# An attention and feed-forward kernel replayed from a step list: the same operations and buffers in a newly fitted order

## The chip, the cores and the metric

The kernel runs on one core of one Trainium2 chip. The metric is the device time of one execution in microseconds, by its median over several executions. A profile shows one single execution, and its span is some 1.8 us shorter than the time of the same execution.

## The reference

Attention with RMS-normed q and k over 8 batches, 12 heads, 448 rows and 64 columns, then a feed-forward block on the 3584 x 768 result:

```python
q_n, k_n = rmsnorm(q, g_q), rmsnorm(k, g_k)
attn = softmax(q_n @ k_n.T / sqrt(64))          # per batch and head
x = (attn @ v).transpose(0, 2, 1, 3).reshape(3584, 768)
h = x @ w_in                                    # 3584 x 2048
g = h * erf(softplus(h))
out = g @ w_out                                 # 3584 x 768
```

## The kernel before

The kernel first records some 2800 operations. Each has a number, the engines that may do it, and the keys that it reads and writes, from which its dependencies follow. Then it replays a step list. A step is a letter for the engine (P TensorE, V VectorE, A ScalarE, G GpSimd, S the sync engine's transfer queue) and the number of the operation. `^n` adds a wait for operation n. `z2*6` is six dummy matmuls on zeros into idle PSUM bank 2.

```python
for step in SCHEDULE.split() or [...]:
    e, what = step[0], step[1:]
    if e == "z":
        bank, n = what.split("*")
        for _ in range(int(n)):
            nc.tensor.matmul(idle[int(bank)], zs[:, 0:P], zs, start=True, stop=True)
        continue
    what, *after = what.split("^")
    o = plan.ops[int(what)]
    o.inst = o.fn(e)
    for d in [*o.sync, *(plan.ops[int(i)] for i in after)]:
        tc.add_manual_dep(o.inst.ins, d.inst.ins.name, must, reason="order")
```

So each engine works through its own steps in the order of the list, whatever else is ready. One unit of four heads begins with four loads into a buffer `raw`, of which there are two. Squares and reduces give the norms:

```python
# four loads per unit: q and k rows 0-383 (384 KB each), q and k rows 384-447
add("S", "ld_raw" if x < 2 else "ld_raw_last", (b, 2 * u, x),
    lambda e, ...: nc.sync.dma_start(dst, src), writes=[key])
# ... twice per unit:
add("G", "sq",  ..., nc.gpsimd.tensor_tensor(sq, part, part, op=ALU.mult), reads=ks, writes=["sq"])
add("V", "red", ..., nc.vector.tensor_reduce(ss[...], sq, ...), reads=["sq"], writes=[("st", si)])
```

The feed-forward products go through two PSUM banks `f` in turn. Each bank is evicted to `ob` (of which there are two as well) and stored:

```python
add("P",  "f2", ..., products, reads=gk + [("wo", n0 // 2)], writes=[("f", fi)])
add("VA", "eo", ..., lambda e: copy(e, osb[oi], fp[:, :JS]), reads=[("f", fi)], writes=[("ob", oi)])
add("S",  "st", ..., lambda e: nc.sync.dma_start(dst, sr), reads=[("ob", oi)])
```

"VA" means that the list chooses VectorE or ScalarE. The first four heads of the first batch are loaded in pairs instead (operations 13 to 20); they are normed, and transposed on TensorE (the first such transpose is P39).

The softmax here doesn't subtract the row's maximum and nothing guards it: scores larger than these inputs give would overflow.

## Time and profile before

| | before |
|---|---|
| time, median of 3 | 472.06 us (471.39 to 472.33) |
| span of the profiled execution | 467.7 us |
| busy TensorE, VectorE, ScalarE, GpSimd | 96, 69, 83, 42% |
| granted TensorE clock | 1.0 |
| TensorE idle | 19.0 us |

A row of the table of costliest groups has, after the bar, busy time and mean ns, and after the second bar the idle time of the engine just before these instructions, with what ended most of it. Two rows, the squares on GpSimd and the reduces on VectorE:

```profile
L320 POOL TENSOR_TENSOR sq<-raw 128x896 f32<-128x896 f32 x42 | 70.5, 1678 | 39.9 <-DMA raw<-in_q_dram 19.0
...
L322 DVE TENSOR_REDUCE st<-sq 128x14 f32<-128x896 f32 x42 | 45.4, 1081 | 16.5 <-POOL sq L320 16.1
```

The squares wait 19.0 us for raw loads, the reduces 16.1 us for squares.

### The profile page before, as it was taken

How to read it: one execution, taken by the hardware profiler on the slowest of the kernel's cores; microseconds unless marked ns; L12 is line 12 of the kernel's file. 1: busy time of each engine (PE TensorE's matmuls, PEld its weight loads, DVE VectorE, ACT ScalarE, POOL GpSimd, SP SyncE). 2: the span in 40 equal slices, each digit the busy share in tenths (PEclk: the TensorE clock that was granted, in tenths of full speed). 3: DMA queues.
4: the chain of work that ended last, by engine and by line, in shares of the span. 5: the costliest groups of instructions: out<-in, count | busy, mean ns of one | idle time of the engine just before them, and what ended most of it. 6: DMA issues, size and time to landing. Idle time of an engine off the chain costs nothing.

```text
span 467.7 us, 7365 instructions
## 1 busy us (share of the span) xinstructions
PE 448.7 (96%) x2579; PEld 221.1 (47%) x2579; DVE 323.2 (69%) x507; ACT 387.7 (83%) x511; POOL 195.1 (42%) x329
## 2 busy tenths in 40 slices
PE   8888999899999998999989999999999999999996
PEld 3334344434554444544454445544455444655663
DVE  3797777798679964797758975698758943284711
ACT  3988999999898988978898897988789886998510
POOL 4467775657562582614552365515370420000000
PEclk9999999999999999999999999999999999999999
DMA  7988999969872447507591377716743022110121
GB/s 166 270 189 163 233 195 173 190 141 189 173 183 85 118 99 217 140 2 189 131 239 52 86 134 168 169 52 154 162 130 87 2 39 67 52 35 18 68 85 68
DMA packets 107893, 59.77 MB, mean 128 GB/s; under 512 B 58576, under 2 KB 107856, under 8 KB 107856
## 3 DMA queue, kind: packets, MB, share of 16 engines
q1 hardware_dynamic: 101440, 52.45, 45.9%
q0 software_dynamic: 5440, 6.29, 9.2%
q10 hardware_dynamic: 976, 0.56, 0.5%
q8 instruction: 20, 0.33, 0.3%
q14 instruction: 17, 0.14, 0.1%
HBM read 45.61 MB, written 11.01 MB: 121 GB/s over the span
## 4 chain that ended last, share of the span: by engine, by line
PE 75%; DVE 7%; DMA 7%; ACT 4%; SPq 3%; POOL 2%; issue 2%; DVEq 0%; POOLq 0%
PE f L657 28%; PE f L707 26%; PE o L543 13%; PE s L466 6%; DMA raw<-in_q_dram 2%; DMA out_dram<-ob 2%; ACT e L509 2%; POOL sq L320 2%; DMA vl<-in_v_dram 2%; PE s L518 1%; DVE g L684 1%; SPq L387 1%; DVE h L275 1%; DVE qk L336 1%; DMA vs<-in_v_dram 1%
## 5 line engine op out<-in xcount | busy, mean ns | idle before, releaser
L657 PE MATMUL f<-xT,w_in_sb 128*128 128x448 bf16 x768 | 163.2, 353 | 3.5 <-DVE h L275 2.9
L509 ACT ACTIVATE e<-s 128x896 bf16<-128x896 f32 x144 | 126.9, 914 | 20.2 <-PE s L466 19.0
L657 PEld LDWEIGHTS <-w_in_sb 128*128 128x128 bf16 x768 | 72.0, 98 | 76.6 <-issue 15.1
L320 POOL TENSOR_TENSOR sq<-raw 128x896 f32<-128x896 f32 x42 | 70.5, 1678 | 39.9 <-DMA raw<-in_q_dram 19.0
L275 DVE COPY h<-f 128x448 f32<-128x448 f32 x101 | 62.0, 620 | 22.7 <-PE f L657 21.4
L606 DVE TENSOR_TENSOR xT<-o,r 64x448 bf16<-64x448 f32 x84 | 52.2, 621 | 35.3 <-ACT r L602 31.4
L543 PE MATMUL o<-e,vm 128*128 128x448 bf16 (+1 forms) x324 | 67.2, 354 | 1.7 <-DVE xT L595 1.4
L707 PE MATMUL f<-w_out_sb,g 128*128 128x384 bf16 x384 | 66.8, 326 | 1.3 <-DVE ob L275 1.2
L707 PE MATMUL f<-w_out_sb,godd 128*128 128x384 bf16 x384 | 65.0, 326 | 2.4 <-DVE ob L275 2.4
L322 DVE TENSOR_REDUCE st<-sq 128x14 f32<-128x896 f32 x42 | 45.4, 1081 | 16.5 <-POOL sq L320 16.1
L275 DVE COPY ob<-f 128x384 f32<-128x384 f32 (+1 forms) x46 | 25.3, 551 | 44.5 <-PE f L707 41.4
L600 ACT ACTIVATE r<-o 64x448 f32<-64x448 f32 x84 | 45.2, 538 | 12.1 <-PE o L543 10.1
L672 ACT ACTIVATE sp<-sp 128x1792 f32<-128x1792 f32 x32 | 52.0, 1687 | 0.1
L668 ACT ACTIVATE sp<-h 128x1792 f32<-128x1792 f32 x31 | 50.4, 1686 | 1.1 <-DVE h L275 1.0
L707 PEld LDWEIGHTS <-godd 128*128 128x128 bf16 x384 | 37.4, 98 | 28.5 <-issue 3.8
L707 PEld LDWEIGHTS <-g 128*128 128x128 bf16 x384 | 37.1, 98 | 28.0 <-issue 3.1
L466 PE MATMUL s<-qT 64*128 64x448 bf16 x288 | 45.9, 356 | 3.8 <-ACT em L527 2.4
L336 POOL TENSOR_TENSOR qk<-raw,st 128x256 bf16<-128x256 f32 x42 | 30.1, 717 | 27.2 <-ACT st L327 18.6
L275 POOL COPY kp<-qT 64x64 bf16<-64x64 bf16 x71 | 21.0, 299 | 46.3 <-PE s L518 33.4
L543 PEld LDWEIGHTS <-vm 128*128 128x128 bf16 (+1 forms) x324 | 25.8, 100 | 30.4 <-issue 10.7
L336 DVE TENSOR_TENSOR qk<-raw,st 128x640 bf16<-128x640 f32 x42 | 36.3, 878 | 3.7 <-ACT st L327 3.3
L275 POOL CAST vm<-vl 128x384 bf16<-128x384 f32 x43 | 24.9, 580 | 30.9 <-DMA vl<-in_v_dram 13.5
(75 smaller groups left out, 441.7 us busy)
## 6 DMA issues: line engine op xcount, KB each, us to landing
vl<-in_v_dram SPq DMA_DIRECT2D x48, 192.0 KB, 3.8
out_dram<-ob SPq DMA_DIRECT2D x47, 192.0 KB, 2.2
raw<-in_k_dram SPq DMA_DIRECT2D x21, 384.0 KB, 4.6
raw<-in_q_dram SPq DMA_DIRECT2D x21, 384.0 KB, 4.7
w_in_sb<-in_moe_w_in_dram POOLq DMA_DIRECT2D x4, 768.0 KB, 7.5
w_out_sb<-in_moe_w_out_dram POOLq DMA_DIRECT2D x8, 384.0 KB, 5.2
out_dram<-ob SPq DMA_DIRECT2D x17, 96.0 KB, 2.2
vs<-in_v_dram SPq DMA_DIRECT2D x16, 96.0 KB, 3.8
```

Source lines behind the costliest of these rows:

```text
L275: return nc.scalar.copy(dst, src) if e == "A" else (nc.vector if e == "V" else nc.gpsimd).tensor_copy(dst, src)
L320: add("G", "sq", (b, 2 * u, x), lambda e, part=part: nc.gpsimd.tensor_tensor(sq, part, part, op=ALU.mult), reads=ks, writes=["sq"])
L322: add("V", "red", (b, 2 * u, x), lambda e, ss=ss, x=x: nc.vector.tensor_reduce(ss[:, 14 * x : 14 * x + 14], sq, axis=AX.X, op=ALU.add), re ...
L336: add(eng, "nq", (b, p, x), lambda e, g=g: (nc.vector if e == "V" else nc.gpsimd).tensor_tensor(qks[qi].rearrange("p g h d -> p h g d")[:, ...
L466: last = nc.tensor.matmul(st[:, i, :S], qT[r, c0 : c0 + P], qq[r], start=True, stop=True)
L509: add("A", "e", (b, p, s), lambda e, e_=e_, st=st: nc.scalar.activation(e_, st[:, :, :S], func=FN.Exp), reads=[("s", sl, 0), ("s", sl, 1), ...
L543: last = nc.tensor.matmul(dst, lhs, rhs, start=(s == 0), stop=(s == 3))
L606: add("V", "x", (b, p, i), lambda e, i=i, mine=mine: nc.vector.tensor_tensor(x[mine, p, :], o_ps[i][mine, :S], r[mine], op=ALU.mult), read ...
L657: last = nc.tensor.matmul(fp[:, :S], w_in_sb[:, kt, f * P : (f + 1) * P], x[:, kt, :], start=(kt == 0), stop=(kt == KT - 1))
L668: add("A", "sp1" if c == order[0] else "sp", (b, c), lambda e, c=c, h=h: nc.scalar.activation(sps[c], h, func=FN.Softplus), reads=[("h", c ...
L672: add("A", "erf1" if c == order[0] else "erf", (b, c), lambda e, c=c: nc.scalar.activation(sps[c], sps[c], func=FN.Erf), writes=[("sp", c, ...
L707: last = nc.tensor.matmul(fp[:, :JS], src[nt // 4][:, nt % 4, col : col + P], w_out_sb[:, nt, js], start=(nt == 0), stop=(nt == NF - 1))
```

## The change

The intent: the list was fitted anew, and the fit now charged work that is planned close behind the landing of a transfer. Only the step list differs. The whole list is replaced; here are its first lines and the stretch around the largest gap.

```diff
-A15 S16 G2 A13 S14 G7 S20 A19 G10 A17 S18 A12 S24 G1 G3 S23 G4 G11 S21 A29 G9 V30 S22 V0 S69 A31 G8 S125 A32 A34 V33
-S28 S27 z0*29 P39 V5 V35 S42 A40 S26 V41 A36 S25 A37 z2*6 P46 V38 P48 A47 S126 G60 A58 z4*3 P66 S124 P50 V67 A49
 [...]
-P1048 S1127 P1049 S1289 A1064 G1092 P1110 A1065 P1111 A1073 S1088 V1320 P1079 G1321^1320 A1072 P1071 S1292 P1112
-A1074 P1113 S1290 P1138 A1114 V1076 G1054 P1139 G1348 A1078 P1140 S1115 V1075 P1128 S1116 P1129 A1080 V846 S1291
-P1081 P1083 A1082 P1130 S1087 V1347 P1084 P1085 S1353 P1086 P1131 S1095 A1102 P1141 S1354 A1101 P1132 G1293 P1133
-S1356 P1142 A1103 P1134 S1355 A1188 P1135 P1143 V1136 P1144 P1145 V1294 P1148 P1149 P1150 V1146 G1295 P1151 P1158
 [...]
+A15 S14 V0 G1 S16 A17 G11 A13 S18 A19 S20 G2 A12 S24 G3 G4 G9 S22 S23 G10 V29 S21 S27 G8 V30 S28 S42 A31 S69 A32 A34
+V33 S25 S125 V35 z0*34 P39 A40 S126 V5 A41 A36 z0*5 P48 A37 S26 P46 V38 A49 S123 A47 V58 S124 z4*4 P66 G43 P52 A60
 [...]
+P1122 G1067 A1043 V1039 P1109 S1290 G1068 P1123 G1062 V1038 P1124 S1289 P1044 P1070 S1292 A1045 P1046 A1077 P1047
+G1093 V1063 P1048 A1125 P1049 P1110 V846 S1126 A1073 P1111 S1291 A1072 P1112 P1113 P1071 A1074 V1114 P1079 P1138
 [...]
+P1134 S1354 P1142 P1135 S1356 P1143 V1136 P1144 P1145 V1302 S1137 G1329^1302 P1148 V1146 G1094 P1149 G1301 P1150
+V1096 G1092^1096 S1147 P1151 A1189 V1105 S1355 P1152 P1153 V1288 S1353 P1158 G1300^1288 V1294 P1159 S1322 P1160
```

In the second stretch S1289 to S1292 are the four loads of batch 4, heads 8 to 11, G1293 is their first square, V1294 its reduce, and V1136 and V1146 are two evictions. The loads move ahead, and the reduce moves from between the evictions to behind both.

## The prediction

> **What bounds the kernel now.** I read the page first: which engine is full, and where it is not.
>
> ```profile
> PE 448.7 (96%) x2579; PEld 221.1 (47%) x2579; DVE 323.2 (69%) x507; ACT 387.7 (83%) x511; POOL 195.1 (42%) x329
> ```
>
> TensorE is busy for 448.7 of 467.7 us, and its granted clock is full in every slice. Only 19.0 us are idle. An order can win idle time back, and shorten the start, where busy time is partly dummy matmuls on zeros (groups of L799: 9.6 + 4.5 + 4.4 = 18.5 us busy, 75 of them). It can't shorten the real matmuls, which are the same ones in both kernels.
>
> Next I asked for busy time by stage, to place those 19 us (columns: stretch, length, then busy us of PE, PEld, DVE, ACT, POOL, the clock, DMA share, GB/s).
>
> ```profile
> 20.00:40.00 20.00, 17.35 (x142) 8.36 (x142) 17.04 (x24) 17.15 (x29) 12.80 (x19) 1.00 0.88 201
> 40.00:60.00 20.00, 18.20 (x120) 7.90 (x120) 14.24 (x21) 18.99 (x33) 15.07 (x22) 1.00 1.11 215
> 60.00:80.00 20.00, 19.43 (x101) 8.39 (x100) 13.95 (x23) 18.22 (x32) 12.11 (x22) 1.00 0.94 179
> 80.00:104.00 24.00, 21.74 (x112) 9.66 (x111) 20.98 (x29) 22.77 (x23) 14.48 (x24) 1.00 0.93 164
> 104.00:180.00 76.00, 75.05 (x422) 36.06 (x421) 60.02 (x93) 68.86 (x98) 44.70 (x70) 1.00 0.64 144
> 180.00:260.00 80.00, 76.41 (x432) 38.01 (x431) 58.21 (x99) 69.31 (x82) 32.01 (x49) 1.00 0.51 131
> 260.00:340.00 80.00, 79.82 (x450) 38.33 (x449) 62.59 (x97) 70.54 (x102) 37.95 (x67) 1.00 0.61 139
> 340.00:410.00 70.00, 70.00 (x406) 36.27 (x404) 38.70 (x68) 61.64 (x74) 16.79 (x28) 1.00 0.23 61
> ```
>
> TensorE idles 2.7 us in 20 to 40, 1.8 + 0.6 + 2.3 = 4.6 in 40 to 104, 1.0 in 104 to 180, 3.6 in 180 to 260, 0.2 up to 340 and nothing up to 410. The rest of the 19 lies in the first 20 us (3.3) and after the last matmul. So from 40 us on an order has 9.2 us to win, and 4.7 of that after 104.
>
> Then the timeline around the largest gap, for what ended it (start us, us, what, and in brackets the idle time before it).
>
> ```profile
> 180.33 4.71 PE L707 MATMUL f<-w_out_sb,godd 128*128 128x384 bf16 x28
> ...
> 183.97 1.68 POOL L320 TENSOR_TENSOR sq<-raw 128x896 f32<-128x896 f32 x1 [6.47 <-DMA raw<-in_q_dram]
> ...
> 185.68 1.09 DVE L322 TENSOR_REDUCE st<-sq 128x14 f32<-128x896 f32 x1 [2.27 <-POOL sq L320]
> ...
> 186.68 0.55 DVE L275 COPY ob<-f 128x384 f32<-128x384 f32 x1
> ...
> 187.28 2.92 PE L707 MATMUL f<-w_out_sb,godd 128*128 128x384 bf16 x17 [2.24 <-DVE ob L275]
> ```
>
> This is the mechanism of the case. A raw q/k load landed at 183.9. GpSimd's square (sq), idle for 6.5 us, waited for it; VectorE's reduce stands behind the square; the eviction of a full PSUM bank (ob) stands behind the reduce in VectorE's program order, though it needs none of this; and TensorE, with two banks f, stands behind the eviction. A late transfer becomes 2.2 us of idle TensorE. The load was issued 178.9 to 179.5, behind two output stores in the sync engine's queue, and landed about 5 us after its issue; the order left only about 3 us of matmuls between its issue and the square.
>
> **What the Trainium skill says.** "Trainium Architecture — The Big Picture", section "Inside one NeuronCore": each engine has its own instruction stream, and they meet only through semaphores. The lines above agree: the copy at 186.68 had its bank ready and still came after the reduce. "DMA: Bandwidth & Descriptors", section "Rules for kernel authors", says to issue a DMA early and wait for it late. The trace has the price of not doing so, and its own latency: from issue to landing 4.6 to 4.7 us in the median for the raw loads of 384 KB, 3.8 for v (vl), 3.1 for the transposes; I use these, not the page's fixed cost. "SBUF — State Buffer", section "SBUF: two separate sides": VectorE with two SBUF inputs and GpSimd exclude each other for a whole instruction. The trace agrees: a norm product (qk) on VectorE, 0.82 us as a rule, took 2.03 at 80.9, while the square ran on GpSimd from 80.58 for 1.67; a g product of 0.95 took 2.06 at 145.7, with a square started at 145.3. So a late square also lengthens VectorE work that the order had placed clear of it.
>
> **The change part by part.** Nothing is added or removed: operations, buffers and dependencies are the same. Three things move.
>
> (1) Loads against first readers. The step list is in order of planned start, so for every load I laid the matmuls between its step and the step of its first reader end to end, with durations from the trace (0.38 us for a pair of 448 columns, 0.325 for a pair of 384, about 0.29 for a score pair). Closer than 5 us stand, in before, 7 of 46 large raw loads, 9 of 42 small ones, 17 of 48 v loads and 14 of 39 transposes, together 47 of 175; in after 1, 0, 2 and 1, together 4. Medians go from 7.5, 7.2, 7.4, 5.6 to 8.8, 8.8, 8.9, 7.4 us. With a landing at 3 to 5 us, this is what should end the gaps. Site by site, from the trace of before and the new order:
> - 184 us (unit batch 4, heads 8 to 11): nearest load 3.1 us ahead before, 5.9 after, and the two evictions now stand before the reduce on VectorE. Gain 2.2.
> - 240 us (batch 5): 3.6 before, landed 237.9, gap 1.2 us; 6.7 after. Gain 1.2.
> - 300 us (batch 7): 3.6 to 5.8, gap 0.3. Gain 0.3.
> - 147 us (batch 4, first unit): its nearest load goes the wrong way, 4.4 to 3.7. The gap of 0.95 us stays, perhaps 0.4 longer. Loss 0.4.
> - 93 us: the square waited behind GpSimd copies for the load of v's last rows, issued 2.3 us of matmuls ahead and now 7.3. The five dummies and the 0.6 us gap there took 1.67 us. Gain 1.2, as VectorE is nearly full in this stretch (20.98 of 24).
> - 78 to 84 us: gaps of 0.34 and 1.43, from copies behind the 2.03 us product. In the new order that product comes 3.4 us before the square instead of 1.1 after it. Gain 1.2.
> - 54 us: the first unit of batch 2 goes from 6.0 to 5.0, and its load took 6.5 in this crowded stretch. Loss 1.0.
> Sum of (1): 2.2 + 1.2 + 0.3 - 0.4 + 1.2 + 1.2 - 1.0 = 4.7 us gained.
>
> (2) The start (first 42 us). The dummies ahead of the first transpose go from 29 to 34. In before the 29th starts at 8.57 and the transpose at 9.37, data ready at 9.31; five more of 0.19 us end near 9.7, so about 0.35 us is lost. The first pair's q load is now issued third on its queue rather than second, its square goes to VectorE (1.0 against 0.95 us on ScalarE): nothing to 0.5 lost. Against that, a small copy of v rows on VectorE that took 1.67 us at 32.9 (others 0.19) and lay on the chain that ended last goes to GpSimd: up to 1.5 gained; and 37 dummies stand after the first transpose instead of 46. Net 0.5 gained, give or take 1.5.
>
> (3) Engines and switches. 22 copies of h go from VectorE to ScalarE and 18 back; net 10 gains of q go to GpSimd, 11 v casts come to VectorE. That is some 4 us on VectorE and 2 on ScalarE out of 323 and 388, spread out: zero on the path. On TensorE a switch between score pairs (64 rows) and other matmuls costs about 0.1 us; from and to f and the main o products there are 164 in both orders, with the early o products 6 more: 0.6 lost.
>
> New collisions of the kind of 147 us can't be counted from the list; I allow 0.6 for them. Sum: 4.7 + 0.5 - 0.6 - 0.6 = 4.0 us. 472.06 - 4 = 468.
>
> **The rivals.** (a) The waits go, and others take their place: TensorE at 96% has no slack, and with loads earlier, buffers must come free earlier, so a load can wait in the sync queue on its old readers (it already waits 25.3 us on qk products), and stores behind it. For it: the list has the gains of q closer to their scores, 8.4 us in the median where it was 12.0. Against it: buffer distances hardly change (norm product to next raw load 5.5 to 5.2). It makes 471 to 473. (b) The start decides: its latencies chain through four engines, and a fit that moves every step there may win or lose 3 us. It alone makes 465 or 471. (c) All gaps of 40 to 410 us go, and the start gains 2: 472.06 - 9.2 - 2 = 461. Against it: the 147 us and 54 us sites go the wrong way. (d) Nothing: the DMA waits are hidden anyway. Against it stands the chain at 184 us, in which no other releaser was late.
>
> **Range and chances.** The middle is 467.5, a little below the sum, since a fit is likely kept when it wins in the stretches that I can't work out. Eight times in ten within 462 to 471.5: all of (1) with 2 more at the start gives the low end, rival (a) the high end. Faster by 2% means under 462.6, that is 9.4 us: more than all idle time from 40 to 410 us, so it needs the start too: 0.12. Slower by 2% (481.5) needs new gaps twice as large as all old ones: 0.02. Same: 0.86.
>
> **What would show it.** Right: TensorE idle in 180 to 260 falls from 3.6 to under 1; the waits of squares on raw loads (19.0 us) and v casts on v loads (13.5 us) fall to less than half; no eviction of ob or h directly behind a reduce that waited for a square; the gap near 147 us (first unit of batch 4) is still there, at about 1 us. Wrong: TensorE's idle time from 40 us on stays near 9 us with other releasers (rival a), or the first f product of batch 0 starts more than 2 us away from its 49.0 (rival b).

## The result and the profile after

| | before | after |
|---|---|---|
| median, runs of the same rounds | 471.73 us (468.70 to 472.33, 4 runs) | 465.67 us (464.64 to 466.58, 4 runs) |
| ratio | | 0.9884, 95% interval 0.9836 to 0.9931 |
| span of the profiled execution | 467.7 us | 462.9 us |

The change is 1.2% faster, which is "same" at a threshold of 2%. A ratio here is the mean time of one kernel's fast runs over that of the other's fast runs of the same rounds, so it is not quite the ratio of the medians quoted beside it. Executions over 1.5% slower than the fastest of the same kernel are left out of the means. The profiled execution of before was one of its faster ones, so the spans differ by less (4.8 us) than the medians (6.1 us).

The line of busy times of the changed kernel, and its busy time by stage (columns as in the prediction):

```profile
PE 450.2 (97%) x2580; PEld 220.4 (48%) x2580; DVE 331.6 (72%) x518; ACT 388.7 (84%) x516; POOL 188.8 (41%) x313
```

```profile
40.00:60.00 20.00, 19.98 (x125) 8.27 (x121) 14.60 (x22) 19.17 (x32) 14.26 (x23) 1.00 1.15 205
...
104.00:180.00 76.00, 74.05 (x414) 35.09 (x412) 63.90 (x96) 67.45 (x98) 39.17 (x59) 1.00 0.71 152
180.00:260.00 80.00, 79.72 (x452) 39.61 (x451) 62.09 (x101) 74.40 (x92) 36.95 (x55) 1.00 0.48 123
260.00:340.00 80.00, 80.00 (x456) 39.59 (x455) 62.23 (x99) 71.62 (x102) 35.31 (x58) 1.00 0.55 141
```

TensorE's idle time is a stretch's length less its busy time. From 40 to 60 it fell from 1.8 us to nothing, from 180 to 260 from 3.6 to 0.3, and from 260 to 340 to nothing. From 104 to 180 it rose from 1.0 to 2.0.

The place of the old largest gap, in the timeline of the changed kernel:

```profile
178.68 7.64 PE L708 MATMUL f<-w_out_sb,godd 128*128 128x384 bf16 x46
...
180.36 1.67 POOL L321 TENSOR_TENSOR sq<-raw 128x896 f32<-128x896 f32 x1
...
181.80 0.56 DVE L276 COPY ob<-f 128x384 f32<-128x384 f32 x1 [1.89 <-PE f L708]
...
182.78 0.56 DVE L276 COPY ob<-f 128x384 f32<-128x384 f32 x1 [0.20 <-PE f L708]
...
184.94 1.09 DVE L323 TENSOR_REDUCE st<-sq 128x14 f32<-128x896 f32 x1
```

The square starts without a wait in brackets: the last of its loads had landed at 177.4. Both evictions wait for TensorE and not the other way round. The reduce comes 2.9 us after the square's end, and TensorE runs on without a gap (46 matmuls up to the end of the window).

The list of waits of the changed kernel (engine, tile, what it waited for: total us, times, longest):

```profile
DVE st L323 <- POOL sq L321: 9.5, 10, 1.8
...
POOL sq L321 <- DMA vl<-in_v_dram: 7.9, 1, 7.9
POOL vm L276 <- DMA vl<-in_v_dram: 7.4, 1, 7.4
...
POOL sq L321 <- DMA raw<-in_q_dram: 4.5, 3, 4.0
POOL sq L321 <- DMA out_dram<-ob: 4.3, 1, 4.3
...
POOL sq L321 <- DMA raw<-in_k_dram: 4.1, 1, 4.1
```

By these labels GpSimd's squares still wait 7.9 + 4.5 + 4.3 + 4.1 = 20.8 us for transfers, against 19.0 (plus 3.4 behind a store) before. But a label can name a transfer that was still under way when the wait ended. The 4.3, and 4.0 of the 4.5, ended just after a reduce on VectorE (at 240.60 and 291.10) that frees the one buffer `sq`. The 7.9 ended at 146.15, 0.3 us after a raw q load had landed (145.84), while the v load of the label landed at 146.88. Put to the landings, raw loads ended 7.9 + 4.1 + 0.4 + 0.2 = 12.6 us of the squares' waits, where before it was 22.5 (the 3.4 ended as a raw q load landed, at 237.90). And the reduces on VectorE wait 9.5 us instead of 16.1, never over 1.8: the waiting of the engine on which evictions stand fell too.

The new order also has a gap that the old one had not, again by the timeline:

```profile
119.06 1.72 POOL L321 TENSOR_TENSOR sq<-raw 128x896 f32<-128x896 f32 x1
119.27 2.32 DVE L685 TENSOR_TENSOR g<-h,sp 128x768 bf16<-128x768 f32 x1
...
121.65 0.82 PE L708 MATMUL f<-w_out_sb,g 128*128 128x384 bf16 x4 [1.01 <-DVE g L685]
```

A square began 0.21 us before a g product with two inputs from SBUF. The product took 2.32 instead of 0.95 us, and TensorE, which needed it, idled 1.01 us. That is the exclusion which the Trainium skill describes ("SBUF — State Buffer", section "SBUF: two separate sides"), and the trace agrees: 0.95 us is the usual time, and 2.32 is close to the rest of the square (1.51) plus 0.95, which is 2.46. The collision does not come in every execution of this order (see `a_guard` below).

The start has a loss and a gain. In the timelines of before and of after, the lines that decide are these:

```profile
5.51 0.95 ACT L408 ACTIVATE sp<-sp 128x896 f32<-128x896 f32 x1 [0.78 <-DMA sp<-in_k_dram]
...
9.37 0.56 PE L371 MATMUL f<-ident,g 128*128 128x128 bf16 x7 [0.45 <-DVE g L419]
...
32.85 1.68 POOL L320 TENSOR_TENSOR sq<-raw 128x896 f32<-128x896 f32 x1 [2.39 <-PE s L466]
32.90 1.67 DVE L275 CAST vx<-vs 64x64 bf16<-64x64 f32 x1
...
34.61 0.62 DVE L595 TENSOR_TENSOR xT<-o,r 128x448 bf16<-128x448 f32 x1
```

```profile
6.93 1.09 DVE L410 TENSOR_TENSOR sp<-sp 128x896 f32<-128x896 f32 x1 [5.82 <-DMA sp<-in_q_dram]
...
10.91 0.56 PE L372 MATMUL f<-ident,g 128*128 128x128 bf16 x7 [0.51 <-DVE g L420]
...
31.56 0.24 POOL L276 CAST vx<-vs 64x64 bf16<-64x64 f32 x1 [1.27 <-PE o L544]
...
32.91 0.62 DVE L596 TENSOR_TENSOR xT<-o,r 128x448 bf16<-128x448 f32 x1 [0.16 <-ACT r L594]
```

The loss: the first pair's square began at 6.93 instead of 5.51, since its q load, now third on its queue, landed at 6.81 instead of 4.69 (the old square then still waited for a k load, landed at 5.41). The first transpose on TensorE came 1.54 us later. The gain: the small cast vx took 1.67 us on VectorE next to a square, and now takes 0.24 us on GpSimd; the product xT behind it came 1.7 us earlier. The first product of the feed-forward block starts at 46.32 instead of 49.04, 2.72 us earlier. Of that, 1.15 us is not a gain: three operations of batch 1 (0.39 + 0.47 + 0.29 us) have moved from ahead of it to behind it. And this is one profile of the new start: in those of `after_again`, `a_late` and `a_guard`, which have the same start, the product starts at 47.76, 47.73 and 48.58.

### The profile page after: what moved, and what is told of

Same layout as the page of the kernel before. It is cut to its first block, busy times and chain, and to the rows that moved or that the text cites.

```text
span 462.9 us, 7382 instructions
## 1 busy us (share of the span) xinstructions
PE 450.2 (97%) x2580; PEld 220.4 (48%) x2580; DVE 331.6 (72%) x518; ACT 388.7 (84%) x516; POOL 188.8 (41%) x313
## 4 chain that ended last, share of the span: by engine, by line
PE 73%; DVE 8%; ACT 6%; DMA 6%; POOL 3%; issue 2%; SPq 1%; ACTq 0%; DVEq 0%; POOLq 0%
PE f L708 29%; PE f L658 25%; PE o L544 12%; PE s L467 6%; DMA sp<-in_q_dram 2%; ACT e L510 2%; DMA out_dram<-ob 2%; DVE h L276 1%; POOL sq L321 1%; PE s L519 1%; ACT sp L673 1%; DVE st L323 1%; DMA raw<-in_k_dram 1%; DVE qk L337 1%; DMA vl<-in_v_dram 1%
## 5 line engine op out<-in xcount | busy, mean ns | idle before, releaser
L321 POOL TENSOR_TENSOR sq<-raw 128x896 f32<-128x896 f32 x42 | 72.1, 1716 | 47.6 <-DVE st L323 24.0
L276 DVE COPY h<-f 128x448 f32<-128x448 f32 x97 | 59.7, 620 | 25.4 <-PE f L658 24.4
L337 POOL TENSOR_TENSOR qk<-raw,st 128x256 bf16<-128x256 f32 x42 | 29.0, 698 | 31.6 <-ACT st L328 20.4
L276 POOL COPY kp<-qT 64x64 bf16<-64x64 bf16 x64 | 16.2, 258 | 56.4 <-PE s L519 40.2
L276 POOL CAST vx<-vs 64x64 bf16<-64x64 f32 x68 | 19.6, 295 | 35.4 <-PE o L544 21.8
```

Source lines behind the costliest of these rows:

```text
L276: return nc.scalar.copy(dst, src) if e == "A" else (nc.vector if e == "V" else nc.gpsimd).tensor_copy(dst, src)
L321: add("G", "sq", (b, 2 * u, x), lambda e, part=part: nc.gpsimd.tensor_tensor(sq, part, part, op=ALU.mult), reads=ks, writes=["sq"])
L337: add(eng, "nq", (b, p, x), lambda e, g=g: (nc.vector if e == "V" else nc.gpsimd).tensor_tensor(qks[qi].rearrange("p g h d -> p h g d")[:, ...
```

## The experiments

All are edits of one of the two step lists. In each diff only the moved steps are shown, with neighbours that did not move; a line of "..." is a cut. Line numbers in the profiles of edited kernels are 7 smaller than in the changed one. There were three calls, each on another chip; the kernel before had 471.0, 471.9 and 472.3 us in them (medians of 11 runs each, a slow one among them in the second and the third). So times of different calls are compared by their ratio to before.

### Which part: the start or the rest (two hybrids, first call; one repeated in the third)

`h_after_start` takes the new order up to the first score product of batch 1 (P314), then the old.

```diff
-A15 S16 G2 A13 ... up to P314 (order of before)
+A15 S14 V0 G1 ...  up to P314 (order of after)
 ... then the order of before
```

> The new order up to the first score product of batch 1 (about 42 us), the old order from there on. Theory (the gain of 4.8 us in the profiled span comes from about 1.5 us at the start, about 1.5 us in 42 to 105 us and about 3.8 us from 180 us on, less 1.5 lost in 105 to 180): 470.2 us, 1.0 to 2.0 under before, and the idle stretches of the old order near 184 and 240 us stay at about 2.2 and 1.2 us. Rival (the start decides, since its chain runs through four engines): 4 us or more under before.

Measured: correct, 469.51 us, ratio 0.9972 (0.9931 to 1.0014). By the mean that is 1.3 us, but the interval holds zero. TensorE's gap near 187 us was still there (2.01 us), as it must be.

`h_before_start` is the other way round: the old start, then the new order.

```diff
 A15 S16 G2 A13 ... up to P314 (order of before)
-... then the order of before
+... then the order of after, with its dummies z6*5 and z7*3
```

> The old order up to the first score product of batch 1, the new order after it. Theory: 3 to 3.5 us under before, no gap over 0.5 us from 180 us on. Rival (the start decides): within 1 us of before.

Measured: wrong result (relative error 0.136), 467.26 us, ratio 0.9915 (0.9889 to 0.9941). The suspicion was that the eight dummies, placed for another order, wrote zeros into a live bank. So the hybrid was run again without them.

```diff
-... P... z6*5 ... z7*3 ...
+... P... ... (no dummies behind P314)
```

> The start of the kernel before up to the first score product of batch 1, then the new order, this time without the two groups of dummy matmuls (8) behind the seam. If those dummies fell on a live bank, the result is now correct; if not, it is wrong again. Time: about what the wrong hybrid gave against before, ratio 0.991 (-4 us), as the 8 dummies took about 1.5 us or less. If the start of the new order is worth the most, it would be near 0.997.

Measured: correct, 466.87 us, ratio 0.9886 (0.9843 to 0.9929), that is 5.4 us. Taking away the dummies alone mended the result, so they did the damage; that they did it through a live bank is the likely way, but was not looked at. A dummy is not a free step: it is placed for one order. Of the whole gain, 6.5 us in the second call (below), some 5.4 belong to what follows the start, and 1.1 to 1.3 to the start; by the intervals neither share is known to better than about 2 us.

### Are late loads enough to explain the gaps? (first call, repeated in the third)

`b_loads` is the old order with nine loads earlier: four of the unit at 184 us, two of the one at 240, three of the one at 300.

```diff
-S1126 G1286 P1048 S1127 P1049 S1289 ... S1292 ... S1290 ... S1291
+S1289 S1292 S1290 S1291 S1126 G1286 P1048 S1127 P1049
 ...
-S1628 P1470 ... S1629 ... S1630
+S1629 S1630 S1628 P1470
 ...
-S2053 P1833 ... S1837 ... S2054 ... S2056 ... S2055
+S2053 S2055 S2056 S2054 P1833 ... S1837
```

> The old order with nine steps moved, all of them raw loads in the sync engine's queue: the four of batch 4, heads 8 to 11, ahead of the two stores; two of batch 5 and three of batch 7 beside the first load of their unit. Theory (late landings make the gaps): the gap of 2.2 us near 184 us, that of 1.2 near 240 and that of 0.3 near 300 go; 3 to 4 us under before. Rival (the gain comes from VectorE's order, evictions ahead of reduces, and the loads' distance alone does little, since stores and loads share a queue): under 1 us.

Measured: correct, 474.72 us, ratio 1.0065 (1.0027 to 1.0103): slower. The gaps at 184 and 240 us were gone, but TensorE now idled 4.03 us up to 299.1. In the chain that ended last, and in the timeline:

```profile
292.43 5.95 DMA out_dram<-ob
```

```profile
298.50 0.56 DVE L269 COPY ob<-f 128x384 f32<-128x384 f32 x1 [5.41 <-DMA out_dram<-ob]
...
299.11 3.10 PE L701 MATMUL f<-w_out_sb,godd 128*128 128x384 bf16 x10 [4.03 <-DVE ob L269]
```

An output store (S1837) now stood behind three loads in the sync queue. It took 5.95 us to land; the same store took 3.75 in the profile of before and 3.63 in that of `b_loads2`, and the median of all such stores is 2.2. The next eviction needs that `ob` buffer, and both banks f filled up behind it. Rival (a) of the prediction is real; the loads of batch 7 had been made early at a store's expense. The stall cost more than its 4 us: the trace has a granted clock of 0.50 for the 3.4 us from 298.4 on, which is an estimated 1.7 us more. All six executions of `b_loads` have a mean clock of 0.992 to 0.995, those of before in this call 0.995 to 1.0.

`b_loads2` is the same without the three loads of batch 7.

```diff
-S1126 G1286 P1048 S1127 P1049 S1289 ... S1292 ... S1290 ... S1291
+S1289 S1292 S1290 S1291 S1126 G1286 P1048 S1127 P1049
 ...
-S1628 P1470 ... S1629 ... S1630
+S1629 S1630 S1628 P1470
```

> The kernel before with six raw-load steps alone moved earlier: four of batch 4 (heads 8 to 11) and two of batch 5. The three of batch 7, behind which an output store had waited, stay where they were. Theory (late raw loads made the gaps at 184 and 240 us, and the earlier trial lost only because a store stood behind the loads of batch 7): both gaps gone, none of 4 us near 295, and 2 to 3.4 us less than before (ratio 0.993 to 0.996). Rival (loads moved early cost elsewhere whatever the store does): ratio 0.999 or above, with new gaps after 184 us.

Measured: correct, 467.29 us, ratio 0.9899 (0.985 to 0.9947), a gain of 4.8 us (2.5 to 7) where 2 to 3.4 was expected. Idle time of TensorE from 180 to 260 us was 0.07 us. So moving six steps of the list gives what the two gaps took (2.2 + 1.2 us) and perhaps more. The stall of 4 us was gone, but even here a store was slow: TensorE idled 1.40 us at 300.9, as a store issued at 294.55 let its buffer go only at 300.28. The profiled execution was the slowest of the six (469.71 us), and shows the mechanism once more where no step was moved: a load of v's last rows landed at 90.17, the square behind its cast started at 90.79 and the reduce at 92.50, and the eviction at 93.50 ended a gap of 2.89 us on TensorE at 94.17; from 95.3 on the granted clock was 0.51 for 3.4 us.

In the same call the whole new order behind the old start (`h_before_start2`) has a ratio of 0.9886. The six load steps, at 0.9899, can't be told apart from it.

### Or is it enough to move what stands behind the wait? (first call)

`b_evict` leaves all loads late and moves three reduces behind the next evictions.

```diff
-V1294 P1148 P1149 P1150 V1146
+P1148 P1149 P1150 V1146 V1294
 ...
-V1633 P1500 ... G1634 ... V1505 P1491 G1641 V1635 ... V1495
+P1500 ... V1505 V1633 G1634 P1491 G1641 ... V1495 V1635
```

> The old order with three reduces (and one square behind them) moved behind the next eviction on VectorE, near 184 and 240 us; every load as late as before. Theory (a late load costs TensorE time only where an eviction stands behind its reduce): the squares still wait for their loads until about 184 and 238 us, but the gaps of 2.2 and 1.2 us go: 3 to 3.5 us under before. Rival (a late landing costs its lateness in any order): gaps as before, within 1 us of before.

Measured: correct, 469.06 us, ratio 0.9948 (0.9917 to 0.9979), 2.5 us. The timeline shows the old wait and what came of it:

```profile
185.24 1.68 POOL L314 TENSOR_TENSOR sq<-raw 128x896 f32<-128x896 f32 x1 [6.21 <-DMA raw<-in_q_dram]
185.30 0.56 DVE L269 COPY ob<-f 128x384 f32<-128x384 f32 x1 [0.36 <-PE f L701]
...
191.52 3.71 PE L701 MATMUL f<-w_out_sb,godd 128*128 128x384 bf16 x20 [1.05 <-DVE ob L269]
```

The square still waited 6.21 us for its load, and TensorE did not care: the eviction at 185.30 ran while the square did. But the unit as a whole stayed late, and 1.05 us of the 2.2 came back at 191.5, where the second reduce of the same unit stood ahead of an eviction. Moving either end of the chain removes the gap; only an early load removes its cause.

### The changed kernel again, and with its loads late (second call)

`after_again` is the changed kernel, unedited.

> The changed kernel itself, for a direct comparison on this chip: 465 to 466.5 us, 4.5 to 6 under before; nothing over 0.5 us idle from 180 us on.

Measured: 465.03 us, ratio 0.9862 (0.9825 to 0.9898).

`a_late` is the new order with six raw loads of the units at 184 and 240 us put back among the same neighbours as in the old order.

```diff
-S1290 ... S1289 P1044 P1070 S1292 ... V846 S1126 ... S1291
+S1289 P1110 V846 S1126 ... S1292 P1071 ... S1290 P1138 ... S1291 P1083
 ...
-S1630 ... S1629
+S1629 P1470 ... S1630 P1480
```

> The new order with six raw loads put back to the old order's distance from their square (four of batch 4, heads 8 to 11; two of batch 5). Theory (a late load costs TensorE only where an eviction stands behind its reduce, and the new order has both evictions ahead of the reduce in batch 4, but not in batch 5): gap near 182 us under 0.5 us, gap near 230 us of 1 to 1.5 us; 1 to 1.5 us over the changed kernel. Rival (distance alone decides): both gaps come back, 3 to 3.5 us over the changed kernel. Second rival (distance does nothing): no difference.

Measured: 465.49 us, ratio 0.9871 (0.9838 to 0.9905), 0.5 us above `after_again` and not told apart from it. Lines of its timeline show why:

```profile
181.32 0.56 DVE L269 COPY ob<-f 128x384 f32<-128x384 f32 x1 [1.89 <-PE f L701]
...
182.30 0.56 DVE L269 COPY ob<-f 128x384 f32<-128x384 f32 x1 [0.19 <-PE f L701]
182.84 1.68 POOL L314 TENSOR_TENSOR sq<-raw 128x896 f32<-128x896 f32 x1 [2.92 <-DVE vx L269]
182.89 1.91 DVE L269 CAST vm<-vl 128x384 bf16<-128x384 f32 x1
```

The square came 1.9 us later than in `after_again` (182.84 against 180.94), but both evictions had run or were running by then. The lateness came back in part: TensorE idled 1.04 us at 188.5, where an eviction came late. Not all of that is the chain through the reduce: the cast of v in VectorE's order took 1.91 us beside the late square, 0.42 in `after_again`. At the other unit a square waited 1.75 us for its load, without a gap. The theory missed here: it put the gap at the other unit, and 1 to 1.5 us on the time. So the new order has two protections at these sites, early loads and evictions ahead of reduces, and without the first it loses about 1 us at one site and nothing at the other. How much the charge on landings is worth by itself over the whole list can't be read from this.

### The new gap at 120 us (second call)

`a_guard` holds the square near 119 us back until the g product (V504) is done.

```diff
-S924 A704 P768 V700 G721 P769 ... V693 V504 P709
+S924 A704 P768 V700 P769 ... V693 V504 G721^504 P709
```

> The new order, in which the square of batch 3, heads 4 to 7 (it started at 119.1 us, 0.2 ahead of a g product of 2.3 us on VectorE) waits for that g product. Theory (the product took 2.3 us instead of 0.95 since the square held what both need): the g product takes 0.95 us, the gap of 1.0 us near 121 us falls under 0.3, 0.7 to 1.2 us under the changed kernel. Rival (TensorE waits for something else there as well): g is short, the time stays within 0.3 us.

Measured: 464.87 us, ratio 0.9855 (0.982 to 0.989). The product took its usual time, and the gap at this place was not there:

```profile
120.97 0.96 DVE L678 TENSOR_TENSOR g<-h,sp 128x768 bf16<-128x768 f32 x1
```

Yet TensorE idled 0.36 and 0.37 us at 126.5 and 133.1, and the time was 0.2 us less than `after_again`, which these runs can't resolve. Nor can the profile show that the guard did it. Without the guard the product took 2.32 us in four profiles (`after`, `a_q0` and the two hybrids with the old start), and 0.96 us in three (`after_again`, `a_late`, `a_swap`), where TensorE idled 0.30 us or less before the matmuls that read the product. The kernel that the guard is compared with, `after_again`, had no collision here in its profiled execution. So the collision is real where it falls, and what its removal is worth stays open.

### The first load at the start (second and third call)

`a_q0` exchanges two loads, so that the first pair's q load (13) goes second on its queue again, as in the old order, and drops five dummies ahead of the first transpose.

```diff
-A15 S14 V0 G1 S16 A17 G11 A13 S18
+A15 S14 V0 G1 S16 A13 G11 A17 S18
 ...
-V35 z0*34 P39
+V35 z0*29 P39
```

> The new order with the first pair's q load issued second and the second pair's third, as in the old order, and 29 dummies ahead of the first transpose instead of 34. Theory (the new order's late first transpose, 10.9 us instead of 9.4, is not on the chain that sets the end of the start; that chain runs through the second and third groups of loads): first transpose near 9.4 us, first f product of batch 0 within 0.5 us of the changed kernel, time within 0.7 us of it. Rival (the start is a chain from the first transpose on): 1.0 to 1.5 us under the changed kernel.

Measured: correct, 462.47 us, ratio 0.9815 (0.9775 to 0.9856), 2.6 us less than `after_again`. My theory here, that the first transpose doesn't lie on the chain that matters, fell. The timeline:

```profile
5.26 1.09 DVE L403 TENSOR_TENSOR sp<-sp 128x896 f32<-128x896 f32 x1 [4.14 <-DMA sp<-in_q_dram]
...
9.24 0.56 PE L365 MATMUL f<-ident,g 128*128 128x128 bf16 x7
```

The first transpose came at 9.24, and the first feed-forward product at 45.21 instead of 46.32 in the profile of the changed kernel and 47.76 in that of `after_again`.

`a_swap` is the exchange alone, with the 34 dummies left.

```diff
-A15 S14 V0 G1 S16 A17 G11 A13 S18
+A15 S14 V0 G1 S16 A13 G11 A17 S18
```

> The changed kernel with the first pair's q load and the load behind which it stood exchanged in the order of issue; unlike in the earlier trial, the 34 dummies ahead of the first transpose stay. Theory (the order of the two loads does it): first transpose at 9.4 to 9.9 us, time within 0.6 us of the earlier trial, about 2 to 2.6 us under the changed kernel (ratio to before 0.982). Rival (the number of dummies did part of it): first transpose above 9.8 us, and 1 us or more of the gain lost.

Measured: 463.63 us, ratio 0.9828 (0.979 to 0.9866). The first transpose was at 9.77, in the expected range; by the ratios to before the time was 0.6 us above `a_q0` (1.2 between the medians, but these are of two calls), the most that was expected, and the intervals overlap. Whether the dummies have a share in it stays open.

`a_best` joins the three edits: exchange, 29 dummies, guard.

```diff
-A15 S14 V0 G1 S16 A17 G11 A13 S18
+A15 S14 V0 G1 S16 A13 G11 A17 S18
 ...
-V35 z0*34 P39
+V35 z0*29 P39
 ...
-S924 A704 P768 V700 G721 P769 ... V693 V504 P709
+S924 A704 P768 V700 P769 ... V693 V504 G721^504 P709
```

> The changed kernel with three edits together: q load of the first pair second, 29 dummies instead of 34, and the square near 119 us held back until the g product beside it is done. If the two gains add, 0.2 to 1 us less than with the start alone: ratio to before 0.980 to 0.981. If small gaps take the place of the one at 120 us, as in the trial of the guard alone, the same as the start alone, 0.9815.

Measured: correct, 462.69 us, ratio 0.9811 (0.9772 to 0.9855), not to be told from `a_q0`. With the guard there were again small gaps: TensorE idled 0.78 us at 124.9 and 0.28 each at 131.5 and 137.1. Its profile is a warning in another way:

```profile
7.23 1.09 DVE L403 TENSOR_TENSOR sp<-sp 128x896 f32<-128x896 f32 x1 [6.11 <-DMA sp<-in_q_dram]
```

With the same order of loads, the q load landed at 5.06 us in the profile of `a_q0`, 5.59 in `a_swap` and 7.03 here; in four profiles of the changed kernel's own start (`after`, `after_again`, `a_late`, `h_after_start`) it landed at 6.81 to 7.62, and at 8.16 in `a_guard`, while in six profiles of the old start it was 4.64 to 4.79. The three kernels with the exchange are at 0.981 to 0.983 of before, the three of the experiments with the new start as it is at 0.9855 to 0.987 (the changed kernel in the first measurement at 0.9884). So the exchange, in two of its three runs with five dummies fewer, is worth some 2 us in the mean. Any two of these profiles could have shown a difference in landing of anything from nothing to 3 us. All three with the exchange have ratios below those of both kernels of the case.

## Why the prediction was right

The time (465.67 us) lies 1.8 us under the predicted 467.5, within the range, and in the class that was given 0.86. The mechanism is shown; that the total came so near is in part luck, since several of its terms were wrong by about 1 us, some on one side and some on the other. Step by step:

- **The mechanism (late load, square, reduce, eviction, TensorE)** is shown from three sides. With early loads alone (`b_loads2`) the gaps at 184 and 240 us go; with the reduces moved alone (`b_evict`) the square waits as before and the gaps go too, in part to come back; with the loads late in the new order (`a_late`) about 1 us of idle time returns, at 188.5, in part by a slowed cast and not resolved in the time.
- **The terms of part (1)**, predicted against measured in the profiles of before and after: 184 us 2.2 and 2.2; 240 us 1.2 and 1.2; 300 us 0.3 and 0.2; 93 us 1.2 and 1.0 (1.11 of dummies and 0.56 of idle before, 0.70 of idle after); 78 to 84 us 1.2 and 0.8 (gaps of 1.77 in all before, 0.95 after). Two had the wrong sign. The site at 147 us should lose 0.4 and gained 0.6 (0.95 before, 0.39 at 154.1 after): its load did come closer, and the square waited 7.9 us (6.6 before) until that load had landed; but this time no eviction that TensorE needed stood close behind. The site at 54 us should lose 1.0 and lost nothing. A short distance in the list is a risk of a wait, and a wait is not yet a cost.
- **New collisions** were put at 0.6. Those found, at 121.65 and 131.59 us, take 1.01 + 0.52 = 1.5. The first is of the kind that the prediction named, though at another place; at the second an eviction waited 1.6 us for a store to free its buffer, the kind of rival (a). In the profile of `after_again` there are 0.57 + 0.30 us at 122.1 and 123.1 instead.
- **Switches on TensorE** were put at 0.6. In the two traces there are 220 such switches instead of 212, and matmuls stand about 0.1 us further apart at each: 0.8.
- **The start** was put at 0.5 gained, give or take 1.5. In the profile of after it gained about 1.6 (2.72 less the 1.15 of moved work); by the same reading the other three profiles of this start give 0.1, 0.2 and -0.7, so the term that was predicted is not refuted. Two terms were mis-sized. The late first transpose was put at 0.35 to 0.85 of loss and cost 1.54 in this profile, and `a_q0` to `a_best` show that some 2 us of time hang on it. Against it the cast vx gave its 1.7, and the two gaps near 44 and 47 us (0.58 and 1.07, where scores waited for ScalarE), which I had not listed, are gone, while new ones stand at 22.4 and 38.6 (1.23 and 1.06). The prediction's sign for rival (b), the first feed-forward product more than 2 us away from 49.0, came true in this profile alone, and only 1.6 us of it is real.
- **The sum**: 2.2 + 1.2 + 0.2 + 0.6 + 1.0 + 0.8 + 0 - 1.5 - 0.8 + 1.6 = 5.3 us. The terms are read from two profiles, and the spans of these differ by 4.8; the medians differ by 6.1. The hybrids divide it alike: 5.4 us for the rest of the list and 1.3, not well resolved, for the start.
- **The stated checks**: TensorE's idle time from 180 to 260 fell to 0.3, as said. The waits of v casts fell from 13.5 to 7.4, not quite to half as said (one wait, at 14.7 us in the start), and those of squares on raw loads from 22.5 to 12.6, put to the landings as above, again not quite to half. This check was badly chosen: it named waits on GpSimd, and the change also kept evictions clear of them. Two evictions do still stand directly behind a reduce that waited for a square (at 73.1 and 191.4 us), without a gap on TensorE. The gap near 147 us, said to stay at about 1 us, became one of 0.39.
- **Slips in the working**, none of which moved the forecast: idle time from 40 us on is 9.35 us by the lines shown, not 9.2; 42 dummies stand behind the first transpose in the new list, not 37; and all of (1) with 2 us more at the start gives 464.9, not the low end of 462.

What stays open: why the landing of the first q load varies by 2 us with one and the same order of loads, whether the new order of the k loads on the sync queue, which no run put back, has a share in the late first transpose, and the share of the early loads alone in the new order's 5.4 us.

## What to carry to other kernels

In a kernel whose engines run in a fixed order, ask of each wait for a transfer what stands behind it on the same engine and on the next one: a wait costs only where an eviction or an operand of the bounding engine stands in that row. It can be mended at both ends, by an earlier load or by moving the needed work ahead of the wait, but an earlier load must not push a store back whose buffer is needed soon. At the start, where nothing else can run, look at the order of the very first loads over several executions; one exchange of two loads was worth some 2 us here, about a third of what the whole fit gained.

## What the Trainium skill lacked or had wrong

- "DMA: Bandwidth & Descriptors", section "Rules for kernel authors", says to issue a DMA early and to wait for it late. The rule has no word of the price. The page does tell elsewhere that a ring takes its transfers in order, but no page gives a figure for what an early load costs those behind it: with three loads moved ahead of an output store, the store landed after 5.95 us (3.75 and 3.63 in two profiles without the move), and TensorE idled 4.0 us (`b_loads`).
- The same page's section "Latency and other measured facts" gives about 2 us of fixed cost for a transfer. No page tells how far a landing varies where many loads start at once: with one order of loads, the first 192 KB of q landed at 5.06, 5.59 and 7.03 us in three executions, and in the old order at 4.64 to 4.79 in six.
- No page tells that a dummy matmul that keeps TensorE busy is tied to the order for which its bank was chosen: eight of them, left in a list whose order had changed, gave a relative error of 0.136, and without them the result was correct.
